# The steps ahead of the first token tile, written in another order, with x split out of PSUM

## The chip, the cores and the metric

One core of one Trainium2 chip runs the whole program. The metric is the device time of one execution in microseconds (us), the median of several. The engines are named as in the profile: PE (matrix multiply, with PEld for its weight loads), DVE (vector), ACT (scalar and activation), POOL (GpSimd), SP (the queue that issues most transfers).

## The reference

Three layers follow one another on 3072 tokens of width 512.

```
attention: q, k, v of (4, 8, 768, 64); 24 chunks of 32 queries per head; a chunk sees its own 32 keys,
           16 to the left, 8 to the right and 8 memory keys;  out = softmax(q k^T / 8) v
x    = attention out as (3072, 512)
xn   = x / sqrt(mean(x^2) + 1e-6) * rms_g
y    = (silu(xn @ w_gate) * (xn @ w_val)) @ w_out          512 -> 1536 -> 512
h    = y @ w_in;  g = h if h >= 1, 0 if h <= -1, else (h + 1)^2 / 4
out  = g @ w_out2                                          512 -> 2048 -> 512
```

## The kernel before

The tokens are worked in six tiles of 512. Attention comes in 24 units `u` (256 tokens of four heads); two units make a pair, 256 tokens of all heads, and two pairs make a tile. Matrix products are done as three passes on split numbers: every operand is a rounded part `hi` plus a rest `lo`, and `mm3` adds hi·hi, hi·lo and lo·hi. So x needs its hi (`xh`) and lo (`xl`) before the first projection, and each weight needs both too.

The change concerns the steps ahead of the first tile. They are written out by hand in the string `ORDER`, and the engines take their instructions in that order. One letter is one step, the number its unit (or its block of 128 tokens):

- `f`: idle matmuls (`fill`, L104) in that number; `s` scores on PE (L426); `m` maximum and subtraction on DVE (L439, L442); `e` exponential on ACT (L451); `a` four transposes on PE (L456); `A` their copy on ACT (L462); `v` product with v on PE (L472); `n` division on DVE (L493 to L499); `q` sums of squares on ACT (L512); `k` two small DVE operations; `p` the root, on POOL (L531); `r` the scaling by root and `rms_g` (L542); `x` four transposes (L552).
- `X` copies a transposed block from PSUM into `xn` (L565). `H` and `L` split `xn` into `xh` (ACT, L354) and `xl` (DVE, or POOL for those in `LO_ON_POOL`, L358), in eight half-tiles each. `G` and `R` are the scaling of pair 0 done by POOL (L685) and ACT (L689) in place of `r`.
- `c`, `d`, `g` convert a unit of weights: `c` reads the loaded 64-bit words on ACT (L133), `d` joins them on DVE (L143, L144), `g` writes hi on ACT (L117) and lo on POOL (L118). A unit is 128 columns of `w_gate`, `w_val`, or 128 rows of `w_out`, in that order by turns; its load (L125, 512 KB) goes through a ring of three buffers, so load n+3 waits until `d` of unit n has read its buffer.

After `ORDER` the first tile begins. For each of 12 blocks `f` of the hidden width PE does 12 matmuls for gate (L579 to L581), 12 for val, and 12 for the output of the block before. Between those groups lie three slots, and in each slot one unit of weights is converted a step further (`conv_w`). From block 1 on PE so needs a new unit about every 12 matmuls. Slots also carry the attention of later tiles. In this first tile PE and SP follow the program's order and the other engines' order is set by the tool's scheduler when the kernel is built; afterwards every engine has the written order.

Of the kernel before, what the change touches and what calls it, by code (L numbers as in the profile page):

```python
# [22 lines left out]


ORDER = """
f15 s0 m0 s1 m1 e0 e1 f4 a0 s2 A0 m2 a1 c0 d0 v0 A1 f6 v1 n0 e2 n1 s3 q0 c1 k0 m3 a2 q1 A2 G0 f4
e3 G1 c2 k1 p0 v2 f1 R1 a3 d1 A3 n2 g0 d2 x1 v3 R0 g1 X1 q2 n3 f7 k2 x0 q3 X0 f1 H4 H6 f3 k3 p1
s4 L4 r2 g2 r3 H0 x2 X2 L0 x3 H2 L6 f3 X3 m4 e4 f4 L2 H1 L1 H5 a4 H3 L5 L3 c3 H7 f1 L7 d3 A4 g3
"""
LO_ON_POOL = ('L0', 'L3', 'L4', 'L6', 'L7')  # L30

TT = 512
PT = 256
# [7 lines left out]
def tile_stream_attention_moe_moe2(  # L41
# [10 lines left out]
    nc = tc.nc  # L52
# [3 lines left out]
    KK = DM // P  # L56
# [8 lines left out]
    att = att_only.enter_context(tc.tile_pool(name="att", bufs=1, side="right"))  # L65
# [11 lines left out]
    xs = poolS("xs", 1)  # L77
# [35 lines left out]
    w1 = {}  # L113
    raw, absd, f32s = [], [], []

    def split(hi, lo, src, eng_lo):
        nc.scalar.activation(hi, src, AF.Copy)  # L117
        eng_lo.tensor_tensor(out=lo, in0=src, in1=hi.bitcast(F32), op=ALU.subtract)  # L118

    def load_w(units, n):  # L120
        for _ in range(n):
            if units:
                dst, key, src = units.pop()
                w64 = wst.tile([P, 1024], U32, tag="w64", name="w64")
                nc.sync.dma_start(w64, src)  # L125
                raw.append((dst, key, w64))
# [23 lines left out]
        join(tu, w64)  # L150
        f32s.append((dst, key, tu))

    def conv_g(eng_lo=nc.gpsimd):
        dst, key, tu = f32s.pop(0)
        w = unit(3 * key[1] + "gvo".index(key[0]))
        split(w[:, 0], w[:, 1], tu.bitcast(F32), eng_lo)
        dst[key] = (w[:, 0], w[:, 1])

    def conv_w():

        n = len(absd)
        if f32s:
            conv_g(nc.vector)
        if raw:
            conv_c()
        if n:
            conv_d()

    units1 = [(w1, ("gvo"[i % 3], i // 3), wts1[i].bitcast(U32)) for i in range(3 * F1)]
# [18 lines left out]
    tt_ = nc.vector.tensor_tensor  # L188
# [147 lines left out]
    m2 = {"single": True, "pace": 0.0, "hold": False}  # L336
# [10 lines left out]
    xhl = {}

    def x_hi(src, kk, part):
        if part.start == 0:  # L350
            xhl[kk] = [
                xs.tile([P, TT], F32R, tag=f"x{hl}{kk}", name=f"x{hl}{kk}") for hl in "hl"
            ]
        nc.scalar.activation(xhl[kk][0][:, part], src[:, kk, part], AF.Copy)  # L354

    def x_lo(src, kk, part, eng):
        hi, lo = xhl[kk]
        eng.tensor_tensor(  # L358
            out=lo[:, part], in0=src[:, kk, part], in1=hi[:, part].bitcast(F32), op=ALU.subtract
        )  # L360

    def split_x(src):
        for kk in range(KK):
            x_hi(src, kk, slice(0, TT))
            x_lo(src, kk, slice(0, TT), nc.vector)


    qk_t = {}
# [27 lines left out]
    def load_v(u):  # L396
        if u >= NU:
            return
        n = 8 * (D + 1)
        if u < 4:  # L400
            if not tails:
                tails.append(xs.tile([P, 4, 2, D + 1], F32, tag="xn", name="v_tail"))
            tail = tails[0][:, u]
            nc.sync.dma_start(tail, v[u].rearrange("p (h c) -> p h c", h=2)[:, :, n - D - 1:])
            vt = [xs.tile([P, TT], F32, tag=f"x{'hl'[hp]}{u}", name="v_in") for hp in range(2)]
            m = n - D - 1
        else:
# [98 lines left out]
    def part_q(u):  # L506
        pr, hh = divmod(u, 2)
        x = x_t[pr]
        ss = small.tile([P, 2], F32, tag="ss", name="ss")
        for blk in range(2):  # L510
            sq = att.tile([P, 4, P], F32, tag="aT", name="sq").rearrange("p g i -> p (g i)")[:, :256]
            nc.scalar.activation(  # L512
                sq, x[blk][:, hh * 256:hh * 256 + 256], AF.Square, accum_out=ss[:, blk:blk + 1]
            )
        ss_t[u] = ss
# [29 lines left out]

    def step_x(pr, blk, ps):
        t, o = divmod(pr, 2)
        if t < 2 and t not in xn_t:
            xn_t[t] = xs.tile([P, KK, TT], F32, tag="xn", name="xn")
        x = x_t[pr]  # L550
        for kk in range(KK):
            nc.tensor.transpose(ps[:, 0, kk * P:(kk + 1) * P], x[blk][:, kk * P:(kk + 1) * P], ident)  # L552
        ps_t["x", pr, blk] = ps

    def part_X(pr, blk):
        t, o = divmod(pr, 2)
# [7 lines left out]
        if pr < 2:
            nc.scalar.activation(xn, rows, AF.Copy)  # L565
        else:
            for kk in range(KK):
                nc.scalar.activation(xn[:, kk], rows[:, kk], AF.Copy, scale=g_t[:, kk:kk + 1])
# [59 lines left out]
    slots = [ps_a] + [spsum.tile([P, 2, 512], F32, name=f"ps_s{i}") for i in range(2)]  # L628
# [2 lines left out]
    load_qk(1)  # L631
    load_v(0)
    load_qk(2)
    load_w(units1, 1)
    load_v(1)
    fns = {"s": step_s, "a": step_a, "v": step_v, "m": part_m, "e": part_e, "A": part_A,
           "n": part_n, "q": part_q, "k": part_k}
    parts = {"s": "me", "a": "A", "v": "nqkp"}
    free = list(range(3))
    use = {}  # L640
    for st in ORDER.split():
        c, n = st[0], st[1:]
        if c == "f":
            fill(slots[free[0]], int(n))
            continue
        n = int(n)
        if c in "savx":
            use[c, n] = free.pop(0)
            ps = slots[use[c, n]]
            if c == "x":  # L650
                step_x(n // 2, n % 2, ps)
            else:
                fns[c](n, ps)
                if n >= 4:
                    done.add(st)
            if c == "s" and n >= 3:
                load_qk(n + 1)
            if c == "v" and n >= 3:
                load_v(n + 1)
            if st == "s0":  # L660
                load_qk(3)
                load_w(units1, 1)
                nc.sync.dma_start(g_b, rms_g.partition_broadcast(P))
                nc.sync.dma_start(g_t, rms_g.rearrange("(k p) -> p k", p=P))
                load_v(2)
                load_w(units1, 1)
                load_v(3)
        elif c == "X":
            part_X(n // 2, n % 2)
            free.append(use.pop(("x", n)))  # L670
        elif c == "r":
            step_r(n // 2, (n % 2,))
        elif c == "p":
            part_p(n)
        elif c in "HL":
            kk, o = divmod(n, 2)
            part = slice(o * PT, o * PT + PT)
            if c == "H":
                x_hi(xn_t[0], kk, part)
            else:  # L680
                x_lo(xn_t[0], kk, part, nc.gpsimd if st in LO_ON_POOL else nc.vector)
        elif c == "G":
            cols = slice(n % 2 * PT, n % 2 * PT + PT)
            for x in x_t[n // 2]:
                nc.gpsimd.tensor_tensor(out=x[:, cols], in0=x[:, cols], in1=g_b[:, cols], op=ALU.mult)  # L685
        elif c == "R":
            pr, blk = divmod(n, 2)
            x = x_t[pr][blk]
            nc.scalar.activation(x, x, AF.Copy, scale=rs_t[pr][:, blk:blk + 1])  # L689
        elif c == "c":  # L690
            conv_c()
        elif c == "d":
            conv_d()
            load_w(units1, 1)
        elif c == "g":
            conv_g()
        else:
            fns[c](n)
            if c in "mAn":
                free.append(use.pop(({"m": "s", "A": "a", "n": "v"}[c], n)))  # L700
# [448 lines left out]
    o1 = Out(F1 // 2, 0, 7, done1, xq)  # L1149
# [130 lines left out]
```

## Time and profile before

| | |
|---|---|
| runs of the kernel | 1160.21, 1160.97, 1162.92 us (median 1160.97) |
| profiled execution | 1161.3 us, its span 1159.5 us |
| mean granted clock of PE | 0.994 of full |
| PE, DVE, ACT, POOL busy, share of the span | 97%, 71%, 53%, 10% |
| first matmul of the first tile | 40.87 us after the span's start |

The span is the stretch from the first to the last instruction of the program; 1.8 us of the execution lie around it. The busy share of PE counts idle matmuls (`f`) and matmuls at a lowered clock as well.

### The profile page before, as it was taken

The numbers are of one execution on the slowest core, as the hardware profiler recorded it, in microseconds if no ns is written. First come the engines' busy times: TensorE is split into PE (matmuls) and PEld (weight loads), VectorE is DVE, ScalarE is ACT, GpSimd is POOL, SyncE is SP. The second block draws the span as 40 slices with busy tenths as digits, with TensorE's granted clock in tenths as the row PEclk, the third lists the DMA queues.
The fourth block names the chain that finished last, engine by engine and source line by source line (L and its number), as shares of the span: only waits on it lengthen the run. The fifth ranks groups of instructions, "written<-read, shape, count | busy, mean of one in ns | idle before, by whom it ended". The sixth has DMA issues, their size and how long they took to land.

```text
span 1159.5 us, 21026 instructions
## 1 busy us (share of the span) xinstructions
PE 1126.5 (97%) x7909; PEld 911.0 (79%) x7909; DVE 821.7 (71%) x1426; ACT 618.8 (53%) x1096; POOL 115.6 (10%) x165
## 2 busy tenths in 40 slices
PE   6889999999999999999999999999999999999998
PEld 4667888777877777887888888788887788887886
DVE  4777767767756666767676867897677887578855
ACT  4677656556566766444444634456444465344553
POOL 2500002223122122101110000000000000000000
PEclk9899999999999999999999999999999999999999
DMA  9766538998979787879997697766777666763564
GB/s 317 236 233 196 187 128 270 298 334 270 305 244 302 256 278 240 289 256 367 407 391 255 212 312 241 220 187 187 233 210 261 181 188 216 221 196 88 162 188 158
DMA packets 144212, 281.81 MB, mean 243 GB/s; under 512 B 15216, under 2 KB 65392, under 8 KB 142320
## 3 DMA queue, kind: packets, MB, share of 16 engines
q1 hardware_dynamic: 123664, 228.57, 60.9%
q0 software_dynamic: 12768, 43.52, 10.9%
q10 hardware_dynamic: 7680, 8.39, 2.1%
q8 instruction: 62, 1.02, 0.4%
q14 instruction: 38, 0.31, 0.1%
HBM read 201.26 MB, written 79.17 MB: 242 GB/s over the span
## 4 chain that ended last, share of the span: by engine, by line
PE 75%; DVE 7%; DMA 7%; ACT 6%; issue 3%; POOL 1%; SPq 0%; ACTq 0%; DVEq 0%; POOLq 0%
PE ps_y L1065 14%; PE ps_g L1065 11%; PE ps_g L579 5%; PE ps_g L580 5%; PE ps_g L581 5%; DMA w<-in_w_dram 3%; PE ps_g L903 3%; PE ps_b L903 3%; PE ps_b L905 3%; PE ps_b L904 3%; PE ps_g L904 3%; PE ps_g L905 3%; PE ps_y L579 3%; PE ps_y L581 2%; PE ps_y L580 2%
## 5 line engine op out<-in xcount | busy, mean ns | idle before, releaser
L1065 PE MATMUL ps_y<-r,wo 128*128 128x512 f32 x672 | 156.2, 390 | 0.0
L579 PE MATMUL ps_g<-xh,wall 128*128 128x512 f32 x384 | 155.7, 405 | 0.0
L581 PE MATMUL ps_g<-xh,wall 128*128 128x512 f32 x384 | 150.8, 393 | 0.0
L580 PE MATMUL ps_g<-xl,wall 128*128 128x512 f32 x384 | 150.6, 392 | 0.0
L1065 PEld LDWEIGHTS ps_y<-r,wo 128*128 128x128 f32 x672 | 125.7, 188 | 26.0
L1015 DVE TENSOR_TENSOR r<-h,r 128x512 fp32r<-128x512 f32 x167 | 112.0, 687 | 44.4 <-ACT r L1013 44.4
L966 ACT ACTIVATE t<-t,half 128x512 f32<-128x512 f32 x96 | 66.9, 720 | 128.3 <-DVE t L965 125.4
L1013 ACT ACTIVATE r<-h 128x512 fp32r<-128x512 f32 x167 | 100.7, 625 | 56.5 <-DVE r L1015 17.5
L1065 PE MATMUL ps_g<-r,wo 128*128 128x512 f32 x498 | 116.0, 390 | 0.0
L1065 PEld LDWEIGHTS ps_g<-r,wo 128*128 128x128 f32 x498 | 93.2, 188 | 19.4 <-DVE r L1015 0.2
L581 PEld LDWEIGHTS ps_g<-xh,wall 128*128 128x128 f32 x384 | 72.6, 189 | 15.8
L579 PEld LDWEIGHTS ps_g<-xh,wall 128*128 128x128 f32 x384 | 72.7, 189 | 15.6
L580 PEld LDWEIGHTS ps_g<-xl,wall 128*128 128x128 f32 x384 | 72.7, 189 | 13.7
L903 PE MATMUL ps_b<-wall 128*128 128x512 f32 x202 | 79.3, 392 | 0.7 <-DVE ps_g L930 0.3
L903 PE MATMUL ps_g<-wall 128*128 128x512 f32 x198 | 78.4, 396 | 1.6 <-DVE ps_y L930 0.7
L904 PE MATMUL ps_b<-wall 128*128 128x512 f32 x202 | 78.7, 389 | 0.0
L905 PE MATMUL ps_b<-wall 128*128 128x512 f32 x202 | 78.6, 389 | 0.0
L579 PE MATMUL ps_y<-hh,wall 128*128 128x512 f32 x192 | 77.6, 404 | 0.0
L904 PE MATMUL ps_g<-wall 128*128 128x512 f32 x198 | 77.1, 390 | 0.0
L905 PE MATMUL ps_g<-wall 128*128 128x512 f32 x198 | 77.1, 390 | 0.0
L581 PE MATMUL ps_y<-hh,wall 128*128 128x512 f32 x192 | 75.1, 391 | 0.0
L580 PE MATMUL ps_y<-hl,wall 128*128 128x512 f32 x192 | 74.9, 390 | 0.0
(201 smaller groups left out, 2104.6 us busy)
## 6 DMA issues: line engine op xcount, KB each, us to landing
wo<-w2o_d SPq DMA_DIRECT2D x88, 512.0 KB, 3.4
wall<-w2p_d SPq DMA_DIRECT2D x168, 256.0 KB, 2.9
wall<-w1p_d SPq DMA_DIRECT2D x84, 256.0 KB, 6.1
w<-in_w_dram SPq DMA_DIRECT2D x36, 512.0 KB, 5.1
w<-in_w_dram POOLq DMA_DIRECT2D x32, 512.0 KB, 5.5
k_in<-in_k_dram SPq DMA_DIRECT2D x48, 256.0 KB, 5.1
wo<-w1o_d SPq DMA_DIRECT2D x21, 512.0 KB, 3.5
v_in<-in_v_dram SPq DMA_DIRECT2D x40, 260.0 KB, 4.2
```

The costliest lines, as they stand in the source:

```text
L579: nc.tensor.matmul(ps, wh, xh, start=start, stop=False)
L580: nc.tensor.matmul(ps, wh, xl, start=False, stop=False)
L581: nc.tensor.matmul(ps, wl, xh, start=False, stop=stop)
L903: nc.tensor.matmul(bank, wh, xh, start=st, stop=False, skip_group_check=True)
L904: nc.tensor.matmul(bank, wh, xl, start=False, stop=False, skip_group_check=True)
L905: nc.tensor.matmul(bank, wl, xh, start=False, stop=kk == 1, skip_group_check=True)
L966: nc.scalar.activation(s, s, AF.Square, scale=0.5, bias=half)
L1013: nc.scalar.activation(r[:, 0], src, AF.Copy)
L1015: tt_(out=r[:, 1], in0=src, in1=r[:, 0].bitcast(F32), op=ALU.subtract)
L1065: nc.tensor.matmul(bank[p][m], a, b, start=s0, stop=s1, skip_group_check=True)
```

## The change

`ORDER` is a new string. Loads of all four first attention units are issued ahead of weights 2 and 3 (the first load of a weight now stands behind the loads of unit 3). The steps `X`, `G` and `R` are gone: a transposed block goes from PSUM straight to `xh` (a copy on ACT, `H`) and `xl` (a subtraction on DVE, `L`), a block of 128 tokens at a time, and pair 0 is scaled by the two `r` steps on DVE. The lo part of a weight becomes a step of its own, `o`, on DVE. POOL keeps the roots `p` and the transfers that it issues. Steps `a` and `A` of unit 4 move into the first tile. The buffers `xh` and `xl` become one tile each; v of the first four units lies in them.

```diff
 ORDER = """
-f15 s0 m0 s1 m1 e0 e1 f4 a0 s2 A0 m2 a1 c0 d0 v0 A1 f6 v1 n0 e2 n1 s3 q0 c1 k0 m3 a2 q1 A2 G0 f4
-e3 G1 c2 k1 p0 v2 f1 R1 a3 d1 A3 n2 g0 d2 x1 v3 R0 g1 X1 q2 n3 f7 k2 x0 q3 X0 f1 H4 H6 f3 k3 p1
-s4 L4 r2 g2 r3 H0 x2 X2 L0 x3 H2 L6 f3 X3 m4 e4 f4 L2 H1 L1 H5 a4 H3 L5 L3 c3 H7 f1 L7 d3 A4 g3
+f15 s0 m0 f4 s1 e0 m1 f3 a0 A0 e1 v0 n0 s2 m2 a1 A1 v1 n1 q0 e2 k0 q1 k1 p0 f2 a2 A2 s3 m3 e3 c0
+r0 f3 v2 n2 a3 A3 r1 x0 H0 d0 q2 k2 v3 n3 q3 x1 H1 k3 p1 L0 g0 f8 r2 r3 L1 x2 H2 x3 H3 s4 o0 c1
+L2 L3 d1 g1 m4 o1 e4 c2 c3 d2 g2 d3 o2 g3 o3 f4
 """
-LO_ON_POOL = ('L0', 'L3', 'L4', 'L6', 'L7')
...
-    def conv_g(eng_lo=nc.gpsimd):
+    def conv_hi():
         dst, key, tu = f32s.pop(0)
         w = unit(3 * key[1] + "gvo".index(key[0]))
-        split(w[:, 0], w[:, 1], tu.bitcast(F32), eng_lo)
+        src = tu.bitcast(F32)
+        nc.scalar.activation(w[:, 0], src, AF.Copy)
         dst[key] = (w[:, 0], w[:, 1])
+        return lambda: tt_(out=w[:, 1], in0=src, in1=w[:, 0].bitcast(F32), op=ALU.subtract)
...
-            vt = [xs.tile([P, TT], F32, tag=f"x{'hl'[hp]}{u}", name="v_in") for hp in range(2)]
+            vt = [x[:, u] for x in v4]
...
     load_qk(2)
-    load_w(units1, 1)
     load_v(1)
...
                 load_qk(3)
                 load_w(units1, 1)
+                load_v(2)
                 nc.sync.dma_start(g_b, rms_g.partition_broadcast(P))
+                load_v(3)
                 nc.sync.dma_start(g_t, rms_g.rearrange("(k p) -> p k", p=P))
-                load_v(2)
-                load_w(units1, 1)
-                load_v(3)
-        elif c == "X":
-            part_X(n // 2, n % 2)
+                load_w(units1, 2)
+        elif c == "H":
+            if not xhl:
+                xh, xl = (xs.tile([P, KK, TT], F32R, tag=tag, name=tag) for tag in ("xh", "xl"))
+                xhl.extend((xh[:, kk], xl[:, kk]) for kk in range(KK))
+            nc.scalar.activation(xh[:, :, n * P:n * P + P], rows(n), AF.Copy)
+        elif c == "L":
+            dst, hi = (x[:, :, n * P:n * P + P] for x in (xl, xh))
+            tt_(out=dst, in0=rows(n), in1=hi.bitcast(F32), op=ALU.subtract)
             free.append(use.pop(("x", n)))
...
         elif c == "g":
-            conv_g()
+            lows.append(conv_hi())
+        elif c == "o":
+            lows.pop(0)()
```

On DVE, around the scaling of pair 1 (`x_nat<-x_nat,rs,g_b`) that the last blocks of x wait for, the order before is this; L358 writes `xl`, L143 and L144 are `d`, L880 is the first product of gate and val:

```order
L521 TENSOR_SCALAR ss<-ss 128x2
L525 SCALAR_TENSOR_TENSOR ss<-ss 128x2
L542 SCALAR_TENSOR_TENSOR x_nat<-x_nat,rs,g_b 128x512 x2
L439 TENSOR_REDUCE m<-ps_s_163 128x8
L442 TENSOR_TENSOR e<-ps_s_163,m 128x2x4x64
L358 TENSOR_TENSOR xl_722<-xn,xh_721 128x256
L358 TENSOR_TENSOR xl_709<-xn,xh_708 128x256
L358 TENSOR_TENSOR xl_654<-xn,xh_653 128x256
L143 TENSOR_SCALAR tu<-tu 128x512
L144 SCALAR_TENSOR_TENSOR tu<-w_360,tu 128x512
```

The same place of the changed kernel has L657 for `xl`, L154 for the lo of a weight, L138 and L139 for `d`:

```order
L510 SCALAR_TENSOR_TENSOR ss<-ss 128x2
L657 TENSOR_TENSOR xl<-ps_s_165,xh 128x4x128
L527 SCALAR_TENSOR_TENSOR x_nat<-x_nat,rs,g_b 128x512 x2
L657 TENSOR_TENSOR xl<-ps_s_164,xh 128x4x128
L154 TENSOR_TENSOR wall<-tu,wall 128x512
L657 TENSOR_TENSOR xl<-ps_a,xh 128x4x128
L657 TENSOR_TENSOR xl<-ps_s_165,xh 128x4x128
L138 TENSOR_SCALAR tu<-tu 128x512
L139 SCALAR_TENSOR_TENSOR tu<-w_254,tu 128x512
```

All four `xl` blocks and the lo of the first weight now stand on DVE behind that scaling, and the second weight (w_254) is joined behind them; before, five of eight `xl` parts and the lo of weights were POOL's.

On ACT, at the first activation of the first tile (the one that reads `ps_g`), the order before has L133 for `c`, L117 for the hi of a weight, L868 for Silu, L594 for the hi of the product:

```order
L133 ACTIVATE tu<-w_562 128x512
L117 ACTIVATE wall<-tu 128x512
L133 ACTIVATE tu<-w_577 128x512
L868 ACT_TABLE_LOAD
L868 ACTIVATE s<-ps_g_111 128x512
L117 ACTIVATE wall<-tu 128x512
L133 ACTIVATE tu<-w_756 128x512
L117 ACTIVATE wall<-tu 128x512
L594 ACTIVATE hh<-s 128x512
```

In the changed kernel the same place reads as follows, with L128, L152, L842 and L576 for the same four:

```order
L128 ACTIVATE tu<-w_256 128x512
L128 ACTIVATE tu<-w_558 128x512
L842 ACT_TABLE_LOAD
L842 ACTIVATE s<-ps_g_111 128x512
L152 ACTIVATE wall<-tu 128x512 x2
L128 ACTIVATE tu<-w_688 128x512
L576 ACTIVATE hh<-s 128x512
L128 ACTIVATE tu<-w_703 128x512
L152 ACTIVATE wall<-tu 128x512
```

The weights before are, in their order, w_188, w_248, w_257, w_360, w_562, w_577, w_756; after, w_244, w_254, w_256, w_558, w_688, w_703, w_708. So ahead of the first Silu ACT had read six units before and reads four now, and the third and fourth unit get their hi behind that Silu (their lo stands on DVE behind the product of gate and val that follows it).

On SP, the loads behind those of the first units stand so before (L404 and L411 load v, L392 k, L393 q, L125 a weight):

```order
L125 DMA w_360<-in_w_dram 128x1024
L392 DMA k_in<-in_k_dram 128x512 x2
L393 DMA q_in<-in_q_dram 128x512
L125 DMA w_562<-in_w_dram 128x1024
L125 DMA w_577<-in_w_dram 128x1024
L411 DMA v_in<-in_v_dram 128x520 x2
L392 DMA k_in<-in_k_dram 128x512 x2
L393 DMA q_in<-in_q_dram 128x512
L125 DMA w_756<-in_w_dram 128x1024
```

And so in the changed kernel (L120 a weight, L377 k, L378 q, L396 v):

```order
L377 DMA k_in<-in_k_dram 128x512 x2
L378 DMA q_in<-in_q_dram 128x512
L120 DMA w_558<-in_w_dram 128x1024
L396 DMA v_in<-in_v_dram 128x520 x2
L377 DMA k_in<-in_k_dram 128x512 x2
L378 DMA q_in<-in_q_dram 128x512
L120 DMA w_688<-in_w_dram 128x1024
L120 DMA w_703<-in_w_dram 128x1024
```

The fifth and sixth unit (w_562, w_577) stood ahead of the loads of attention unit 5; their like (w_688, w_703) now stand behind them, and those wait until the scores of unit 4 are done.

## Rows read from the trace of the kernel before

**Rows 1.** Windows: busy us (instructions) per engine, granted PE clock, DMA share, GB/s.

```profile
25.00:28.00 3.00, 3.00 (x73) 2.05 (x72) 2.17 (x7) 2.81 (x7) 1.47 (x1) 0.50 1.03 386
31.00:35.50 4.50, 0.12 (x5) 0.00 (x0) 2.87 (x1) 1.15 (x4) 4.48 (x7) 0.97 0.97 316
36.00:41.90 5.90, 5.79 (x22) 4.24 (x22) 4.34 (x8) 4.67 (x11) 1.79 (x3) 0.50 0.15 56
60.00:80.00 20.00, 16.43 (x194) 12.82 (x193) 15.11 (x29) 13.33 (x21) 0.00 (x0) 1.00 0.71 235
```

**Rows 2.** The page: engines; a queue of instruction fetches (packets, MB, share).

```profile
PE 1126.5 (97%) x7909; PEld 911.0 (79%) x7909; DVE 821.7 (71%) x1426; ACT 618.8 (53%) x1096; POOL 115.6 (10%) x165
...
q8 instruction: 62, 1.02, 0.4%
```

**Rows 3.** The chain that ended last, 0 to 60 us: start, us, what.

```profile
13.21 1.20 issue
...
17.00 2.07 issue
...
23.45 0.67 issue
...
26.29 1.12 PE ps_s L472 x64
...
51.70 6.27 DMA w<-in_w_dram
```

**Rows 4.** Groups by line, 0 to 41 us: busy us, mean ns, idle before.

```profile
L542 DVE SCALAR_TENSOR_TENSOR x_nat<-x_nat,rs,g_b 128x512 f32<-128x512 f32 x2 | 4.2, 2154 | 1.8 <-POOL rs L531 1.8
L118 POOL TENSOR_TENSOR wall<-tu,wall 128x512 fp32r<-128x512 f32 x3 | 4.0, 1335 | 2.2 <-ACT wall L117 2.1
...
L358 POOL TENSOR_TENSOR xl<-xn,xh 128x256 fp32r<-128x256 f32 x4 | 3.3, 833 | 3.9 <-ACT xh L354 3.9
...
L462 ACT ACTIVATE aT<-ps_s 128x512 f32<-128x512 f32 x4 | 2.4, 592 | 0.7 <-PE ps_s L472 0.5 <-PE ps_s L456 0.2
...
L442 DVE TENSOR_TENSOR e<-ps_s,m 128x512 f32<-128x512 f32 x3 | 2.1, 691 | 0.1
...
L117 ACT ACTIVATE wall<-tu 128x512 fp32r<-128x512 f32 x3 | 1.9, 617 | 0.0
```

**Rows 5.** Timeline of DVE, ACT and POOL, 14 to 32 us: start, us, instruction.

```profile
14.86 0.43 DVE L143 TENSOR_SCALAR tu<-tu 128x512 uint32<-128x512 uint32 x1 [0.94 <-ACT tu L133]
15.32 0.69 DVE L144 SCALAR_TENSOR_TENSOR tu<-w,tu 128x512 uint32<-128x512 uint32 x1
...
27.55 0.17 DVE L493 TENSOR_SCALAR rd<-ps_s 128x8 f32<-128x8 f32 x1 [0.71 <-ACT wall L117]
...
27.97 0.41 ACT L512 ACTIVATE sq<-x_nat 128x256 f32<-128x256 f32 x1
27.98 0.76 DVE L499 TENSOR_TENSOR x_nat<-ps_s,rd 128x256 f32<-128x256 f32 x2
...
28.82 0.19 ACT L512 ACTIVATION_READ_ACCUMULATOR sq<-x_nat 128x1 f32 x1
...
31.88 0.71 POOL L531 TENSOR_TENSOR rs<-ss,nhalf 128x2 f32<-128x2 f32 x1
```

**Rows 6.** Timeline, 40 to 50 us: start, us, instruction, idle before it.

```profile
40.87 0.85 PE L579 MATMUL ps_g<-xh,wall 128*128 128x512 f32 x1
...
42.48 9.54 SPq L125 DMA_DIRECT2D w<-in_w_dram  x5
...
43.66 1.28 ACT L868 ACT_TABLE_LOAD   x1
...
46.57 0.66 ACT L133 ACTIVATE tu<-w 128x512 f32<-128x512 f32 x1 [0.49 <-DMA w<-in_w_dram]
...
46.99 0.39 PE L579 MATMUL ps_g<-xh,wall 128*128 128x512 f32 x1
...
49.71 0.39 PE L579 MATMUL ps_g<-xh,wall 128*128 128x512 f32 x1
```

More of the change, by code (lines that the diff above doesn't have):

```diff
@@ L114, in tile_stream_attention_moe_moe2 @@
     raw, absd, f32s = [], [], []
-    def split(hi, lo, src, eng_lo):
-        nc.scalar.activation(hi, src, AF.Copy)
-        eng_lo.tensor_tensor(out=lo, in0=src, in1=hi.bitcast(F32), op=ALU.subtract)
     def load_w(units, n):
@@ L162, in conv_w @@
         if f32s:
-            conv_g(nc.vector)
+            conv_hi()()
         if raw:
@@ L345, in tile_stream_attention_moe_moe2 @@
     bg = list(reversed(steps))
[L347 to L360, printed above, removed]
+    v4 = [xs.tile([P, KK, TT], F32, tag=tag, name="v_in") for tag in ("xh", "xl")]
+    xhl = []
     def split_x(src):
-        for kk in range(KK):
-            x_hi(src, kk, slice(0, TT))
-            x_lo(src, kk, slice(0, TT), nc.vector)
+        for kk, (hi, lo) in enumerate(xhl):
+            nc.scalar.activation(hi, src[:, kk], AF.Copy)
+            tt_(out=lo, in0=src[:, kk], in1=hi.bitcast(F32), op=ALU.subtract)
     qk_t = {}
@@ L510, in part_q @@
         for blk in range(2):
-            sq = att.tile([P, 4, P], F32, tag="aT", name="sq").rearrange("p g i -> p (g i)")[:, :256]
+            sq = att.tile([P, 512], F32, tag="e" if u < 4 else "aT", name="sq")[:, :256]
             nc.scalar.activation(
@@ L547, in step_x @@
         t, o = divmod(pr, 2)
-        if t < 2 and t not in xn_t:
+        if t == 1 and t not in xn_t:
             xn_t[t] = xs.tile([P, KK, TT], F32, tag="xn", name="xn")
@@ L563, in part_X @@
         rows = ps[:, 0, :].rearrange("p (k i) -> p k i", k=KK)
[L564 to L568, printed above, removed]
+        for kk in range(KK):
+            nc.scalar.activation(xn[:, kk], rows[:, kk], AF.Copy, scale=g_t[:, kk:kk + 1])
         if t >= 2:
@@ L639, in tile_stream_attention_moe_moe2 @@
     free = list(range(3))
-    use = {}
+    use, lows = {}, []
+    rows = lambda n: slots[use["x", n]][:, 0, :].rearrange("p (k i) -> p k i", k=KK)
     for st in ORDER.split():
@@ L674, in tile_stream_attention_moe_moe2 @@
             part_p(n)
[L675 to L689, printed above, removed]
         elif c == "c":
@@ L783, in slot @@
             after.clear()
-    xn_t.pop(0)
     pend = None
```

## The prediction

> **What bounds the kernel now.** The page comes first: PE is busy 97% of the span, the next engine 71% [rows 2]. So what a change ahead of the first tile can give is PE time that is empty or slow there, and what it can take is PE time that goes empty in the tile behind it. The first matmul of the first tile starts at 40.87 [rows 6]; the windows show an empty PE from 31.0 to 35.5 (0.12 us busy of 4.5) and a PE at 1.2 GHz, half the full clock, from 25 to 28 and again from 36 to 41.9, the second time right behind that gap [rows 1]. The chain of waits names what else holds the stretch: 1.20 us at 13.21, 2.07 at 17.00 and 0.67 at 23.45 in which PE waits for nothing that the profile shows ("issue") [rows 3]. They stand inside runs of small attention matmuls, about as many PE instructions apart each time. The page has 62 transfers in an instruction queue for 7909 matmuls and 7909 weight loads [rows 2], some 255 instructions for each, so I read these stops as PE waiting for its next block of instructions. Last, the first tile itself: from 60 to 80 PE is empty for 3.57 us [rows 1], and there the chain runs through a transfer of weights that takes 6.27 us [rows 3]. Already at 46.57 ACT waits for a load that was issued at 42.48 [rows 6]. So weights are short in that tile, and time won ahead of it need not stay won.
>
> **The blocks of instructions.** Ahead of the tile the changed PE program has as many scores and products as before, and ten idle matmuls fewer. If the blocks arrive when they did (14.4, 19.1 and 24.1, the ends of the three waits), they stop other steps: `v` of unit 0 now runs ahead of the first stop, but `s` of unit 2 meets it; the second is still near the end of `v` of unit 1, the third near the end of `v` of unit 2. So that product ends near 24.45 in both kernels, and all earlier edits (loads in another order, `A0` ahead of `e1`, unit 0's product earlier) are worth nothing for the start of the tile; the blocks cover them. Without that cover they would be worth some 4 us, which is a rival below.
>
> **From 24.45 to the tile.** Division of unit 2 takes 1.19 (27.55 to 28.74 for its like [rows 5]): 25.65. `v` of unit 3 at half clock takes 1.12 [rows 3]: 26.8. `H0` must wait for it, since x lies where v lay; it costs 0.6 (a 128x512 copy out of PSUM [rows 4]): 27.45. Squares of unit 2 are next on ACT, 1.04 (27.97 to 29.01 [rows 5]): 28.5; DVE holds its small sum ahead of unit 3's division, so that runs from 28.7 to 29.9. Squares of unit 3 start after its first half and end at 30.55, sum and root 0.2 + 0.71 [rows 5]: 31.5.
>
> Here the change gains most. Before, the two scalings behind the root took 2.15 each, while POOL ran its subtractions of 0.83 and 1.34 [rows 4]; the same form with nothing on POOL took 0.69 [rows 5]. With POOL at roots alone I take 0.69 twice: 32.9. The price of the contention is so 2 x 1.46 = 2.9 us of this path; the bounds are 0 and 2.9, and I take the upper, as the row of 0.69 is DVE alone.
>
> Then the last transposes (0.6 from 32.9), `H3` 0.6 and its `L`. DVE has L1, the lo of the first weight, L2 and L3 behind the scaling, 0.69 each [rows 4]: 32.9 + 2.8 = 35.7. Idle matmuls and scores of unit 4 fit beside that. First matmul of the tile: **35.7, 5.1 us earlier**. Of these 2.9 are the contention; the rest is that x needs no `xn` and no half-tile pieces.
>
> **What the tile gives back.** A projection is 12 matmuls, 2.72 us (46.99 to 49.71 [rows 6]). Gate of block 0 runs 35.7 to 38.4, val to 41.15 at full clock. Two queues now stand differently. DVE: join of unit 2 (0.43 + 0.69 [rows 5]) to 36.8, `m4` 1.4, lo of unit 2 at 38.9, just in time. ACT: exponential of unit 4, two reads of 0.66, a table load of 1.28 [rows 6], Silu 0.6: 42.15, then hi of the third and fourth weight: 43.4. DVE: product 42.9, two lo parts: 44.25. Block 1's gate needs the fourth weight: PE ends val at 41.15 and can't do its first matmul before 43.4, its third before 44.25. **PE waits 2.3 + 0.4**; gate ends near 46.5, where it ended at 49.7 before [rows 6].
>
> The fifth weight is issued after unit 2's join, at 36.9, lands near 41 (4.0 for the one issued at 42.48 [rows 6]) and is read at 43.4 to 44.1. But its hi stands on ACT behind the read of the sixth, issued at 40.75 and landing at 44.75. Read, hi and lo follow: 47.9. PE, after unit 4's transposes (moved in, 0.6), needs it at 47.6: 0.35 more. Val of block 1 ends at 50.2, before at 49.71 + 2.72 = 52.4. Left of the 5.1: **2.2 us**.
>
> From there the pattern is the old one: three buffers, one unit a slot. The 3.57 us of waits at 60 to 80 [rows 1] I take as unchanged; the bounds are that they vanish (-3.6) or double (+3.6), and the units' distance to PE is nearest to before's.
>
> The clock is the open term. Before, the half clock covered the tile's first 1 us and cost some 0.7 (gate and val of block 0 took 46.99 - 40.87 = 6.12 instead of 2 x 2.72 = 5.44 [rows 6]). In the new order PE has gaps of about 2.4 and 1.7 us between 27 and 33. If a low stretch like 36 to 41.9 falls on the start of the tile, its matmuls run at half rate for up to 6 us, which moves the product, and the lo parts behind it, by up to 2.4; without one nothing is lost. I take 0.5, between these. Sum: 2.2 - 0.5 = 1.7 us less. The profiled execution is 1161.3, so 1159.6; it stands 0.3 above the median of the runs, so **1159.3**.
>
> **Rivals.**
> - *Instruction blocks don't hold the new order.* Loads of units 2 and 3 arrive earlier, and if PE is not stopped, unit 1's product ends near 14.7, unit 2's near 18.5 and unit 3's near 21.5, as v of unit 3 has landed by then; the tile starts near 31.5, 4.2 earlier than in my sum, and most of it stays since the conversion steps move along: 1155.5. The three waits speak against it, the emptier DMA queue behind the first weights for it. The Trainium skill ("Runtime: NRT & Kernel Launch", section Instruction fetch mechanics) says that fetches come in 256-instruction blocks and that crossing one is mostly hidden; the trace agrees on the size, not on the hiding. By that rule this rival would hold. Chance 0.15.
> - *The weights come late: slower.* The price is the sixth weight. If it lands not 4.0 but 6.27 after its issue, as the one in the chain did [rows 3], the fifth's hi is 2.3 later and so is PE; if then the waits at 60 to 80 double, because the ring enters the tile with two units fewer ahead, 3.6 more: 2.2 - 2.3 - 3.6 is 3.7 slower, 1164.7. It decides from a landing near 47 on. For it: ACT waits for loads here already; against: the queue is idle at 40 in my order. Chance 0.20.
> - *The change doesn't end the slow scalings.* If the 2.15 is no matter of POOL's work, 2.9 of the 5.1 are gone, and the tile gives back less, about half, since its conversions stand behind the same scalings: 1160.8, within 0.2%. Against it: 0.69 for the same form. Chance 0.10.
>
> **How the numbers follow.** My case has 0.55. 0.2% of the median is 2.3 us, about what a measurement of this kernel can tell from no change; so faster means under 1158.65. My case reaches from 1157 (no low clock, a little less waiting) to 1161.5 and lies on both sides: 0.27 faster, 0.28 same. Faster 0.27 + 0.15 = 0.42; same 0.28 + 0.10 = 0.38; slower 0.20. The range goes from 1156.0 to 1163.5 and cuts the far half of the first two rivals; my case alone is 1157 to 1161.5.
>
> **What would show it.** Right: scalings (L527) of 0.7 each; first `ps_g` matmul at 34 to 37; "issue" waits in `s` of unit 2 and `v` of units 1 and 2; PE empty for 2 to 3 us ahead of block 1's gate. Wrong: "issue" waits gone and the tile at 32; L527 at 2; PE waiting for weights beyond 80, where it hardly waited before; or half clock through the tile's first 6 us.

## The result and the profile after

The changed kernel takes 1167.74 us (median of 12 runs, 1165.16 to 1173.59) against 1161.91 us before (12 runs): ratio 1.0058, 95% interval 1.0039 to 1.0076. It is slower by some 6 us, and the range forecast, 1156.0 to 1163.5, doesn't hold it. The profiled execution has a span of 1163.4 us, 3.9 more than before. A trace is of one run alone: the changed kernel's is of its fastest (1165.16 us), those of e4 and e5 below are of their slowest (1168.31 and 1167.54 us).

The page's row of engines, which answers to [rows 2], tells nothing of it:

```profile
PE 1126.7 (97%) x7899; PEld 909.7 (78%) x7899; DVE 820.4 (71%) x1433; ACT 614.3 (53%) x1086; POOL 103.1 (9%) x152
```

The windows do. Here are those of the start and one at 505 us, columns as in [rows 1]:

```profile
13.00:25.00 12.00, 8.10 (x271) 5.73 (x272) 5.36 (x14) 4.72 (x13) 0.72 (x1) 0.72 0.97 315
25.00:28.00 3.00, 1.96 (x73) 1.46 (x72) 2.24 (x5) 2.02 (x6) 0.00 (x0) 1.00 0.41 145
28.00:34.90 6.90, 5.13 (x83) 3.26 (x83) 5.68 (x13) 3.75 (x10) 1.45 (x2) 0.75 0.46 156
35.00:41.00 6.00, 5.72 (x26) 4.39 (x24) 5.15 (x10) 4.10 (x6) 1.48 (x3) 1.00 0.95 323
60.00:80.00 20.00, 16.36 (x134) 13.00 (x133) 15.03 (x30) 14.13 (x24) 1.07 (x1) 1.00 0.77 262
505.00:520.00 15.00, 10.83 (x42) 8.51 (x41) 4.38 (x9) 3.64 (x7) 1.98 (x3) 0.89 0.74 262
```

And the same last window of the kernel before:

```profile
505.00:520.00 15.00, 15.00 (x68) 12.25 (x67) 7.46 (x14) 6.18 (x12) 2.29 (x4) 1.00 0.96 348
```

From 505 to 520, far behind every step that the change moves, PE is empty for 4.2 us and at half clock for a part of the rest. The start itself went almost as forecast. PE's timeline of the changed kernel, 12 to 48 us:

```profile
14.54 0.83 PE L411 MATMUL ps_s<-k_in,q_in 64*32 64x64 f32 x61 [2.07 <-issue]
...
19.20 0.37 PE L457 MATMUL ps_a<-v_tail,aT 64*32 64x65 f32 x2 [1.15 <-issue]
...
23.95 0.26 PE L457 MATMUL ps_a<-v_in,aT 64*32 64x65 f32 x4 [0.33 <-issue]
...
34.95 0.51 PE L561 MATMUL ps_g<-xh,wall 128*128 128x512 f32 x1
...
42.25 0.50 PE L561 MATMUL ps_g<-xh,wall 128*128 128x512 f32 x1 [1.53 <-ACT wall L152]
...
43.13 0.50 PE L563 MATMUL ps_g<-xh,wall 128*128 128x512 f32 x1 [0.15 <-DVE wall L154]
...
47.12 0.50 PE L563 MATMUL ps_g<-xh,wall 128*128 128x512 f32 x1 [0.52 <-DVE wall L154]
```

The tile starts at 34.95 (forecast 35.7, before 40.87) and then waits 1.53, 0.15 and 0.52 for weights. The two scalings of pair 1, 2154 ns each before [rows 4], take 1.41 together:

```profile
31.21 1.41 DVE L527 SCALAR_TENSOR_TENSOR x_nat<-x_nat,rs,g_b 128x512 f32<-128x512 f32 x2 [0.17 <-POOL rs L516]
```

The loss is in one place. The timeline of the changed kernel at 505 us, where four tiles are through and the last two are taken up as a pair (`product`, L877; `ys` is the output of the fourth tile, `y_d` its place in DRAM):

```profile
505.35 0.32 SPq L596 DMA_DIRECT2D y_d<-ys  x1
...
505.95 0.58 ACT L896 ACTIVATE ps_g<-ps_g 128x512 f32<-128x512 f32 x1 [1.44 <-PE ps_g L879]
...
511.66 0.60 ACT L897 ACTIVATE t<-ps_b 128x512 f32<-128x512 f32 x1 [5.13 <-DMA y_d<-ys]
...
513.42 0.69 DVE L904 TENSOR_TENSOR ps_b<-t,ps_g 128x512 f32<-128x512 f32 x1
...
514.16 0.79 PE L877 MATMUL ps_g<-wall 128*128 128x512 f32 x1 [4.17 <-DVE ps_b L904]
```

The same three instructions of ACT and DVE before:

```profile
507.17 0.32 SPq L614 DMA_DIRECT2D y_d<-ys  x1
...
509.13 0.60 ACT L923 ACTIVATE t<-ps_b 128x512 f32<-128x512 f32 x1 [0.78 <-PE ps_b L905]
...
510.89 0.69 DVE L930 TENSOR_TENSOR ps_b<-t,ps_g 128x512 f32<-128x512 f32 x1
```

Read from the bottom: PE waits for DVE, DVE for ACT's copy into `t`, and ACT 5.13 us for a store to land. Before, the copy waited for nothing but its product, though the store stood at the same point of the program and landed later still (at 514.02, against 511.56 in the changed kernel). Nothing in the arithmetic ties `t` to `y_d`; what ties them is memory. The pool `xs` (xn, x, v) is closed there and the next pool lies over it. The addresses of the built programs, in bytes behind the start of `xs`, with the old tenant ahead of the bar and the new one behind it:

```
                   before                    changed
     0 to  8192    xn, ys  | r0 r1           xh      | r0 r1
  8192 to 16384    x tiles | r2 r3           xl      | r2 r3
 16384 to 24576    x tiles | r4 t0 t1        xn, ys  | r4 t0 t1
```

Places are given in the order in which buffers are first asked for. Before, that was `v_tail` (in the buffer xn) and then v of unit 0. The change asks for `v4`, the two whole tiles, first; so `xn`, and in it `ys`, moved from the front to the back, under the `t` that is handed out first:

```
        m2["n"] += 1
        return m2["t"][m2["n"] % len(m2["t"])]
...
        p5 = tmp2("p5")
        nc.scalar.activation(B, A, AF.Copy)
        nc.scalar.activation(p5, C, AF.Copy)
```

### The profile page after: what moved, and what is told of

Read it like the earlier page. It is cut to its first block, busy times and chain, and to the rows that moved or that the text cites. A ratio compares the mean times of both kernels' runs of the same rounds, so it can differ in the third digit from the quotient of the medians.

```text
span 1163.4 us, 20975 instructions
## 1 busy us (share of the span) xinstructions
PE 1126.7 (97%) x7899; PEld 909.7 (78%) x7899; DVE 820.4 (71%) x1433; ACT 614.3 (53%) x1086; POOL 103.1 (9%) x152
## 4 chain that ended last, share of the span: by engine, by line
PE 48%; DVE 5%; ACT 2%; issue 1%; DVEq 0%
PE ps_y L1039 14%; PE ps_g L1039 11%; PE ps_g L877 3%; PE ps_b L877 3%; PE ps_b L879 3%; PE ps_b L878 3%; PE ps_g L879 3%; PE ps_g L878 3%; PE ps_y L877 2%; PE ps_y L879 2%; PE ps_y L878 2%; ACT t L940 2%; DVE h L944 1%; DVE t L939 1%; PE ps_y L1075 1%; DVE t L908 1%
## 5 line engine op out<-in xcount | busy, mean ns | idle before, releaser
L877 PE MATMUL ps_g<-wall 128*128 128x512 f32 x198 | 78.9, 399 | 5.7 <-DVE ps_b L904 4.2
L877 PE MATMUL ps_b<-wall 128*128 128x512 f32 x202 | 79.5, 393 | 0.7 <-DVE ps_g L904 0.3
```

Of the source, the lines that this page charges most:

```text
L877: nc.tensor.matmul(bank, wh, xh, start=st, stop=False, skip_group_check=True)
```

## The experiments

Theory A: this placement makes the loss, and the new steps by themselves gain what was forecast. Rival B: the new steps lose the time and the wait at 505 us is only where it shows. Ratios are to runs of the kernel before on the same chip, with 95% intervals; in the expectations "the fifth run" is e5, and so on, and theories C to J are named where they come up. e8 was run once and has no ratio.

| run | median us | ratio |
|---|---|---|
| changed kernel | 1167.74 | 1.0058 (1.0039 to 1.0076) |
| e1_xn_front | 1162.53 | 0.9997 (0.9978 to 1.0016) |
| e2_t_ring | 1163.08 | 1.0006 (0.9987 to 1.0025) |
| e3_before_xn_back | 1168.45 | 1.0044 (1.0025 to 1.0062) |
| e4_lo_on_pool | 1164.16 | 1.0001 (0.9983 to 1.0019) |
| e5_v_ahead_of_x | 1160.72 | 0.9978 (0.9958 to 0.9997) |
| e6_before_v_ahead | 1160.73 | 0.9974 (0.9956 to 0.9992) |
| e7_need_order | 1161.49 | 0.9985 (0.9970 to 0.9999) |
| e9_two_more_buffers | 1159.76 | 0.9966 (0.9946 to 0.9986) |
| e10_later_tile | 1161.58 | 0.9989 (0.9970 to 1.0008) |
| e11_buffers_need | 1156.58 | 0.9943 (0.9923 to 0.9962) |
| e12_buffers_later | 1157.89 | 0.9951 (0.9933 to 0.9969) |

**e1_xn_front.** xn back in front:

```diff
+    tails = [xs.tile([P, 4, 2, D + 1], F32, tag="xn", name="v_tail")]
     v4 = [xs.tile([P, KK, TT], F32, tag=tag, name="v_in") for tag in ("xh", "xl")]
...
-    tails = []
...
-            if not tails:
-                tails.append(xs.tile([P, 4, 2, D + 1], F32, tag="xn", name="v_tail"))
```

> The changed kernel with one edit: the buffer xn (v_tail, later ys) is allocated ahead of xh and xl, as in the kernel before, so that ys no longer lies where t0 and t1 of the next pool come to lie. Theory A (placement): ACT's first copy into t1 waits no more for the last store y_d (5.13 us of ACT, 4.17 us of an empty PE and half a clock behind it near 510 us in the changed kernel); all else stays, with the first tile some 2 us ahead. Expected 1159.5 us, 1158 to 1161, ratio to before 0.998. Rival B: the loss is that of the new front steps, whose 2 us shift puts transfers later in the way, and some other wait takes the place: 1166 to 1169, as the changed kernel.

Measured: 0.9997. The copy waits 0.78 for its product, as before, and PE is busy for all of the 15 us from 505 to 520 (the timeline of SP and ACT, e1_xn_front):

```profile
505.80 0.32 SPq L594 DMA_DIRECT2D y_d<-ys  x1
...
507.76 0.60 ACT L895 ACTIVATE t<-ps_b 128x512 f32<-128x512 f32 x1 [0.78 <-PE ps_b L877]
```

The loss is gone, so rival B falls for the 5 us. But the kernel is now equal to the one before, not 2 us faster (1158 to 1161 was expected): the second half of theory A is in doubt.

**e2_t_ring.** The buffers stay as in the changed kernel; only the first `t` is another:

```diff
     second_pool(F1 // 2, 5, 5, "ring t wo h")
+    m2["n"] = 1
```

> The changed kernel with its buffers where they are, but the ring t of the next pool starts at t2 instead of t1. Theory A: the first copy writes t2, which lies over hh and not over ys; t0 and t1 come some microseconds later, when the store has landed. Expected 1159.5 us, 1158 to 1161.5, as the first run. Rival C: it is the place of the buffers as such (neighbours, banks) and not this one wait: 1166 to 1169 here, though the first run is fast. Rival B: 1166 to 1169 in both.

Measured: 1.0006. One line that touches nothing but which buffer is first gives the same as the move of the pool, and the copy waits 0.78 for its product again. It is this one wait, not the places as such (rival C falls). Like e1, it stays above what was expected, here 1158 to 1161.5 (the timeline of SP and ACT, e2_t_ring):

```profile
506.79 0.32 SPq L596 DMA_DIRECT2D y_d<-ys  x1
...
508.75 0.60 ACT L897 ACTIVATE t<-ps_b 128x512 f32<-128x512 f32 x1 [0.78 <-PE ps_b L879]
```

**e3_before_xn_back.** The kernel before, with its buffers in the changed kernel's order:

```diff
     tails = []
+    v4 = [[xs.tile([P, TT], F32, tag=f"x{hl}{u}", name="v_in") for hl in "hl"] for u in range(4)]
...
-            vt = [xs.tile([P, TT], F32, tag=f"x{'hl'[hp]}{u}", name="v_in") for hp in range(2)]
+            vt = v4[u]
```

> The kernel before with one edit: the eight tiles that hold v and then xh and xl are allocated ahead of xn, so that ys lies over t0 and t1 of the next pool, as in the changed kernel; ORDER is the old one. Theory A: the first copy into t1 waits for y_d (issued at 507, landing near 514, 6.9 us), PE goes empty for some 4 to 5 us near 512 and runs at half clock behind it: slower than before by 6 to 8 us, 1168 to 1170. Rival B: the placement costs nothing by itself: 1161.9, as before.

Measured: 1.0044, with the old ORDER untouched. Its timeline shows the same wait:

```profile
507.20 0.32 SPq L615 DMA_DIRECT2D y_d<-ys  x1
...
514.76 0.60 ACT L924 ACTIVATE t<-ps_b 128x512 f32<-128x512 f32 x1 [6.38 <-DMA y_d<-ys]
...
517.26 0.79 PE L904 MATMUL ps_g<-wall 128*128 128x512 f32 x1 [5.42 <-DVE ps_b L931]
```

The wait is there and the kernel is slower, by somewhat less than the 6 to 8 us expected. With e1 and e2 this settles the placement from both sides: taken away it is worth 5.2 us by the medians (1167.74 - 1162.53) and 7.1 by the ratios (1.0058 - 0.9997), put in 5.6 by the medians (1168.45 - 1162.85, before in those runs) and 5.1 by the ratio; so 5 to 7 us.

**e4_lo_on_pool.** e1 with POOL at work again while DVE scales:

```diff
-r0 f3 v2 n2 a3 A3 r1 x0 H0 d0 q2 k2 v3 n3 q3 x1 H1 k3 p1 L0 g0 f8 r2 r3 L1 x2 H2 x3 H3 s4 o0 c1
+r0 f3 v2 n2 a3 A3 r1 x0 H0 d0 q2 k2 v3 n3 q3 x1 H1 k3 p1 L0 g0 o0 f8 r2 r3 L1 x2 H2 x3 H3 s4 c1
...
-            lows.pop(0)()
+            lows.pop(0)(nc.gpsimd.tensor_tensor if n == 0 else tt_)
```

> The first run's kernel, with the lo of the first weight moved from DVE to POOL, so that POOL subtracts from about 31.2 us on, while DVE scales pair 1. Theory D (the slow scalings of the kernel before are POOL's work beside them): the first scaling takes 2.0 to 2.2 us instead of 0.7, the second 0.7 to 2.2 by what is left of POOL's 1.3 to 2.2 us; first matmul of the first tile 0.7 to 2 us later than in the first run (one 0.69 step less on DVE counts against it), time 0 to 1.5 us longer. Rival: the scalings were slow for another reason; they stay at 0.7 and the tile starts 0.7 us earlier.

Measured: 1.0001, and of the two scalings at 31 us the second is slow, not the first as expected. The view of the line (minimum, median and longest duration in ns, first and last start) and POOL's timeline, e4_lo_on_pool:

```profile
L525 DVE SCALAR_TENSOR_TENSOR x_nat<-x_nat,rs,g_b x4: 740/748/1758, 23.0 to 31.9; 128x512 f32<-128x512 f32 x4
```

```profile
31.28 1.80 POOL L154 TENSOR_TENSOR wall<-tu,wall 128x512 fp32r<-128x512 f32 x1
```

The scaling that starts at 31.9 takes 1758 ns and ends at 33.66, 0.58 behind POOL's end at 33.08: it stood for most of POOL's subtraction and ran then. In e1, with nothing on POOL there, both take 1.41 together. So POOL's work beside it makes a scaling slow; that the two of 2154 ns before were slow by the same is the plain reading. The Trainium skill ("SBUF — State Buffer", section Who interferes with whom) calls the ports that the two engines share an exclusive lock, over which a DVE instruction with two inputs in SBUF and a POOL instruction that reads SBUF contend; this row agrees (1758 ns behind POOL's start, some 740 for the scaling just ahead of it). The tile starts 0.8 later than in e1 (36.77 against 35.99), and the time didn't move beyond its interval of some 2 us, which can't tell 0.8 from nothing.

So the question became where the lead goes. Starts of the same large matmuls (gate, val, out, counted from the first tile's first) in the traces, in us:

| trace (its run, us) | 1st (tile) | 49th (out of block 0) | 121st (out of block 2) | 1249th (third tile) | first product of the pair |
|---|---|---|---|---|---|
| before (1161.30) | 40.87 | 53.31 | 75.99 | 383.82 | 506.21 |
| e3 (old steps, 1170.17) | 42.15 | 54.06 | 77.38 | 383.81 | 506.24 |
| e6 (old steps, 1163.50) | 40.62 | 52.54 | 78.75 | 384.06 | 506.45 |
| changed (1165.16) | 34.95 | 50.40 | 73.15 | 381.98 | 504.39 |
| e1 (new steps, 1161.99) | 35.99 | 52.22 | 74.01 | 382.46 | 504.84 |
| e2 (new steps, 1163.10) | 36.33 | 52.40 | 76.17 | 383.39 | 505.83 |
| e5 (new steps, 1167.54) | 37.87 | 53.38 | 79.39 | 388.38 | 510.82 |

Means of three and of four: the new steps are ahead by 41.21 - 36.29 = 4.9 at the tile, 53.30 - 52.10 = 1.2 at the 49th, 1.7 at the 121st (in traces that differ by 6 among themselves), and by nothing at the 1249th. But this last hangs on e5's trace: without it the lead is 5.5, 1.6, 2.9, 1.3 and, at the first product, 1.3. The trace of e4 is like e5's (390.16 at the 1249th). In these two PE waits long for ACT's copy `aT` in the attention of later tiles; here e5 and before, PE's waits from 80 to 165 us:

```profile
PE ps_a L455 <- ACT aT L445: 3.8, 2, 2.6
...
PE ps_a L472 <- ACT aT L462: 0.4, 2, 0.2
```

It is 4.6 in e4, 1.4 in e3 and e6, and 0.7 to 1.7 in the changed kernel, e1 and e2. Of e1 and e2 the lead goes behind 506 us: near 590 PE waits 1.0 and 1.5 for the weights of a product (not in the trace before, but 1.6 in e6), and the 401st product starts at 598.83 and 599.84, before at 598.05. So no single place eats the lead in all traces, and what decides it no run here shows. Two places were tried for it: a wait for v at 254 us (1.9 us before, 3.2 in e1), and the weights of the first tile.

**e5_v_ahead_of_x and e6_before_v_ahead.** The load of the next x goes behind the slot, the same edit on both sets of steps:

```diff
-            if 0 < t < NS - 1 and f == 9:
-                load_x(t + 1)
...
             slot(t, 3 * f)
+            if 0 < t < NS - 1 and f == 9:
+                load_x(t + 1)
```

> The first run's kernel (xn in front) with one more edit: the load of x for the next tile (1 MB) is issued behind the slot of its block instead of ahead of it, so the v of the next attention unit stands ahead of it in the queue. Theory E (the lead of the new front steps, 1.8 us at 237 us in the first run, is eaten at 254 us, where PE waits 3.2 us for a v that lands at a time set by the queue): v lands some 3 us earlier, the wait falls below 1 us, 2 to 3 us less: 1159.5 us, 1158.5 to 1161. Rival F: later waits for transfers (products' weights near 590 us) take the lead instead: 1162 to 1163, as the first run.

> The kernel before with the same edit alone (load of x behind the slot). Its wait for v at 254 us is 1.9 us, and 1 us of half clock follows it. Theory E: 1 to 3 us less than before, and 1 to 2 us more than the fifth run, as the lead of the new front steps counts once nothing eats it: 1160 to 1161.5. Rival F: 1162 to 1163, and no difference to the fifth run.

Measured: 0.9978 and 0.9974. The waits of PE from 240 to 262 us are empty in both, and both gain some 0.2%, which theory E said of each. That e5 would then be 1 to 2 us below e6 it also said, and that is wrong: they are equal. The lead is not what that wait ate. In e5's trace it is gone at the 121st matmul already (79.39); PE's waits ahead of that, 30 to 80 us (us in total, times, longest):

```profile
PE ps_a L439 <- ACT e L434: 5.0, 1, 5.0
...
PE ps_g L561 <- DVE wall L154: 1.4, 1, 1.4
```

**e7_need_order.** e5 with the weights in PE's order:

```diff
-    units1 = [(w1, ("gvo"[i % 3], i // 3), wts1[i].bitcast(U32)) for i in range(3 * F1)]
+    need = sorted(range(3 * F1), key=lambda i: 3 * (i // 3) + i % 3 + (i % 3 == 2) * 2.5)
+    units1 = [(w1, ("gvo"[i % 3], i // 3), wts1[i].bitcast(U32)) for i in need]
```

> The fifth run's kernel with the units of weights in the order in which PE uses them (gate, val of a block, then out of the block before) instead of gate, val, out of one block. In the first tile PE waits 1.5 + 0.7 us for weights ahead of block 1 in the changed kernel; the unit needed there is now the third, not the fourth, and the one after it the fourth. Expected: the waits for weights up to 48 us sum to 1 us instead of 2.2, no new ones; time 1 us below the fifth run if the lead lives on, else the same.

Measured: 0.9985. Waits for weights up to 48 us are 1.0, as expected, but the wait for unit 5's exponential is 5.1 (2.3 before, 2.7 in the changed kernel, 1.7 in e1). So the waits ahead of block 1 are not the bound either, as far as this trace shows; what is short comes later. ACT's timeline of e5 ahead of that exponential (L434) shows it:

```profile
68.19 0.67 ACT L128 ACTIVATE tu<-w 128x512 f32<-128x512 f32 x1 [1.13 <-DMA w<-in_w_dram]
...
70.73 0.67 ACT L128 ACTIVATE tu<-w 128x512 f32<-128x512 f32 x1 [0.83 <-DMA w<-in_w_dram]
71.42 1.28 ACT L434 ACT_TABLE_LOAD   x1
72.71 0.63 ACT L434 ACTIVATE e<-e 128x512 f32<-128x512 f32 x1
```

and the changed kernel's (L436):

```profile
65.34 0.66 ACT L128 ACTIVATE tu<-w 128x512 f32<-128x512 f32 x1 [0.41 <-DMA w<-in_w_dram]
66.02 1.28 ACT L436 ACT_TABLE_LOAD   x1
67.31 0.63 ACT L436 ACTIVATE e<-e 128x512 f32<-128x512 f32 x1
```

The exponential stands in ACT's order behind the read of a weight, and this read waits for the load. The twelfth weight lands at 62.1 us in the kernel before, at 61.9 in the changed one, 63.0 in e1 and e2, 66.3 in e5: no more than 0.2 earlier, though the tile starts earlier.

**e8_fewer_loads.** e1 without the loads of v of units 2 and 3, so that it leaves out a part of attention; one run:

```diff
+        if u in (2, 3):
+            v_t[u] = v_t[u - 2]
+            return
```

> The first run's kernel without the loads of v for units 2 and 3 (they use the v of units 0 and 1 instead, so part of attention is not computed); 1.05 MB less in the queues up to 21 us. PE's three waits for its next instructions end at 13.75, 19.23 and 25.12 us in the first run. Theory G (the instructions come behind the data in the same queues): the second and third end 1 to 3 us earlier. Rival: each takes its own time after the block before it: within 0.5 us of the first run. Also the first tile starts 1 to 3 us earlier by G.

PE's timeline, e8_fewer_loads:

```profile
12.82 0.83 PE L412 MATMUL ps_s<-k_in,q_in 64*32 64x64 f32 x61 [0.76 <-issue]
...
19.12 0.37 PE L458 MATMUL ps_a<-v_tail,aT 64*32 64x65 f32 x2 [3.30 <-issue]
```

The first stop ends 0.9 earlier than in e1, the second where it did (19.23), now after 3.30 us of waiting, and the third is gone. Neither theory gives that, and 0.9 is no more than traces differ: with all loads the first stop ends between 13.10 (e11) and 14.54 (changed), and e4 has no third stop either. The tile starts at 35.89, against 35.99, so fewer loads didn't start it earlier in this trace. What the stops wait for the traces do show: in the instruction queue a transfer of 16384 bytes ends 1.2 to 1.6 us ahead of the end of each of these stops, in every trace (at 12.84, 17.76 and 22.66 before, for 14.41, 19.07 and 24.11; at 11.49 and 17.58 in e8, for 12.82 and 19.12). In e8 the second of these starts at 16.58, in e1 at 16.73; what sets that time stays open.

**e9_two_more_buffers.** e5 with the fifth and sixth weight in xn, which the new steps leave empty in the first tile:

```diff
-                w64 = wst.tile([P, 1024], U32, tag="w64", name="w64")
+                w64 = bufs[i] if bufs else wst.tile([P, 1024], U32, tag="w64", name="w64")
...
+                wx = xs.tile([P, 2, 1024], U32, tag="xn", name="w64")
+                load_w(units1, 2, [wx[:, i] for i in range(2)])
...
-            load_w(units1, 1)
+            if s >= 2:
+                load_w(units1, 1)
```

> The fifth run's kernel (xn in front, v ahead of x) with two more buffers for weights in the first tile: the fifth and sixth unit are loaded into the buffer xn, which stands empty from the end of unit 3's product to the second tile, right behind that product; the ring of three then goes on with the seventh. Theory H (the lead of the new front steps dies in the first tile because the weights come at the pace of a ring of three: the twelfth unit lands at 62.1 us in the kernel before and at 61.9 to 66.3 with the new steps, though the tile starts 3 to 6 us earlier): the fifth and sixth land near 33 us instead of 42 to 47, the twelfth 2 to 5 us earlier than in the fifth run, PE's wait for unit 5's exponential near 70 us falls from 5.0 to below 2, and the time is 2 to 4 us less than the fifth run's, ratio to before 0.994 to 0.996. Rival I: the transfers as such are full in this stretch, so the later units land no earlier; only the waits ahead of block 1 go, time within 1 us of the fifth run, ratio 0.997 to 0.998.

Measured: 0.9966, 1 us below e5's median and not the 2 to 4 of theory H. The fifth and sixth land at 35.4 and 36.7 (45.5 and 47.3 in e5), the twelfth at 61.1 (66.3); the wait for the exponential is 3.9, not below 2. The twelfth is 5 earlier than in e5 but only 1.0 earlier than in the kernel before, so rival I has a part: two buffers more help the first weights and hardly those at 60 us. The traces can't carry more: e1 has the program of e5 in the first tile, and there the twelfth lands at 63.0 and the wait is 1.7.

**e10_later_tile.** e5 with a later start, by idle matmuls at the end of ORDER:

```diff
-L2 L3 d1 g1 m4 o1 e4 c2 c3 d2 g2 d3 o2 g3 o3 f4
+L2 L3 d1 g1 m4 o1 e4 c2 c3 d2 g2 d3 o2 g3 o3 f24
```

> The fifth run's kernel with 20 more idle matmuls ahead of the first tile, which starts some 2.9 us later (20 x 0.147). Theory H (weights set the pace in the first tile, not its start): the later start costs little, the twelfth unit lands when it did within 1.5 us, and the time is 0 to 1 us more than the fifth run's. Rival J: PE bounds the first tile and the lead is lost further on: 2 to 3 us more.

Measured: 0.9989 against 0.9978, 0.9 us more by the medians. By theory H 0 to 1, by rival J 2 to 3; the intervals of some 0.2% each don't part the two. Nor do the traces: the start is 2.0 behind e5's (39.88) but the 1249th matmul 4.7 ahead of it (383.67); beside e7, which differs from e5 in the order of weights alone, they are 2.9 and 1.3 behind (36.97 and 382.33).

**e11_buffers_need and e12_buffers_later.** e11 has the edits of e7 and e9 together on e5; e12 is e11 with the `f24` of e10.

> The run with two more buffers, and besides the weights in the order in which PE uses them. If the waits for weights in the first tile are then gone, the time is 0 to 1 us below that run; by rival I the same as the seventh run.

> The eleventh kernel (two more buffers, weights in PE's order) with 20 more idle matmuls ahead of the first tile, as in the tenth run. Theory H, carried on: with weights two units further ahead the start of the tile sets its end again, so the 2 to 3 us count: ratio to before 0.9943 + 0.0015 to 0.0025, 0.996 to 0.997, some 2 us more than the eleventh. Rival: weights still set the pace at 60 to 75 us, and the later start costs below 1 us: 0.994 to 0.995.

Measured: e11 0.9943 (0.9923 to 0.9962), 1156.58 us, the fastest here: 3 us below e9, where 0 to 1 was expected. PE's waits, 36 to 140 us, e11_buffers_need:

```profile
PE ps_a L440 <- ACT e L435: 2.6, 1, 2.6
PE ps_a L456 <- ACT aT L446: 1.6, 2, 0.9
PE ps_g L562 <- DVE wall L154: 1.0, 1, 1.0
```

On e5's 1160.72 the order alone gives nothing (1161.49), the buffers alone 1.0 us, both 4.1; why they need each other was not taken apart, and the order was not tried on the old steps, so what part the new steps have in it isn't known. e12 costs 0.0008 more by the ratios, 0.9 us, and 1.3 by the medians, for a start that was to be 2.9 later and is 4.6 later in the traces (41.16 against 36.53; at the 121st matmul 74.49 against 74.28, at the 1249th 380.54 against 377.80). That lies between the rival's "below 1 us" and theory H's 2, and inside the intervals.

## Why the prediction was wrong, step by step

- **The blocks of instructions: right.** The three stops stand in unit 2's scores and in the products of units 1 and 2, as forecast, after the same numbers of matmuls as before (221, 348, 475 in both traces), and end at 14.54, 19.20 and 23.95 (14.4, 19.1, 24.1 before). The rival in which they don't hold, with a tile at 31.5, is out.
- **From 24.45 to the tile: right.** 35.7 forecast, 34.95 in the trace and 34.95 to 37.87 in four; 5.1 us earlier forecast, 4.9 by the means. The price of the contention, 2.9, was right in size (2 x 2154 ns against 1.41 us) and, by e4's one slow scaling, in cause. The third rival is out.
- **What the tile gives back, up to block 1: right in kind, small in size.** Forecast waits of 2.3 + 0.4 and 0.35, measured 1.53 + 0.15 and 0.52. The lead there is 2.9 in the changed kernel's trace and 1.2 by the means (1.6 without e5), for 2.2.
- **"From there the pattern is the old one": it held in the changed kernel's trace, and the times don't bear it out; the smaller of two errors.** The waits at 60 to 80 were taken as unchanged, with the lead kept. In the changed kernel's trace that came out: PE is empty there for 3.64 us (3.57 before), and it is 1.8 ahead at the first product (504.39 against 506.21), close to the sum's 2.2 - 0.5 = 1.7. But with equal placement the new steps are worth nothing that can be measured: e1 against before 0.9997, e2 1.0006, the changed kernel against e3 1.0058 and 1.0044, e5 against e6 0.9978 and 0.9974. The interval of e1 alone would still hold a gain of 1.7 us; that four comparisons have none on the mean speaks against it. The lead was lost in different places (80 to 165 us, near 590 us), none of which the prediction looked at; why stays open. That weights pace the first tile is in part argued: the twelfth lands when it did. The rival "weights come late" had this mechanism, with a price of 3.7 on the wrong side that no run shows.
- **What was not in the sum at all: the larger error.** "xh and xl become one tile each" stands in the change and got no line in its cost part by part. So the step that failed is a term put at nothing without a reason. The edit moves xn by 16384 bytes, a copy at 506 us gets a store to wait for, and that costs 5 to 7 us (e1, e2, e3): 4.17 us of an empty PE, then matmuls at a clock of 0.76 on average from 515 to 520 us. No rival held it. Without it, e1 and e2 (1162.53 and 1163.08) lie inside the range forecast, but beside a kernel before of 1162.85, so not by the sum's gain. Ahead of the run, the wait could have been seen from the addresses or from what ACT waits for at that copy in both built programs; the price from the store's 6.9 us to landing (issued 507.17, landed 514.02 before), against a copy that came 2 us behind the issue.
- **The clock:** it was low ahead of the tile (0.72 on average from 13 to 25, 0.75 from 28.0 to 34.9) and not on the tile (1.00 from 35 to 41) in the changed kernel's trace; in e5 the first matmuls of the tile did run slow (0.53 from 38 to 40, matmuls 0.43 apart). The 0.5 was no more than a middle.

## What to carry to other kernels

A new shape or order of buffers is a change of its own: list what will lie over each when its pool is closed, and which store or read then stands between the old tenant and the new, however far from the edit. Time won ahead of a long stream need not reach its end: here 4.9 us at the tile were 1.2 to 1.6 at the 49th matmul, 1.3 at 506 us in three traces, and nothing in the times, while two more buffers for weights, together with the order of need, took 4.1 us off e5. That a lead counts once the weights get ahead too would fit this, but it isn't shown. A lead of a microsecond or two is to be followed in several traces: one trace of four turned it to nothing here. A stall may be tested from both sides cheaply: take it out of the new kernel in two ways and put it into the old one.

## What was not expected of the hardware

PE's three stops for instructions come after 221, 348 and 475 matmuls in the traces of both kernels, each 1.2 to 1.6 us behind the end of a transfer of 16384 bytes in the instruction queue, and PE stands for them: the second cost from 1.15 (changed) to 3.30 us (e8). The wait of 4.17 us at 510 us was followed by matmuls 0.43 us apart (514.75 to 515.18) instead of 0.23, so that the stall costs about 1.4 times its length: 5.8 us of lead were lost around it in the changed kernel's trace, from 1.8 ahead of the kernel before to 4.0 behind. In e3 it is about 1.5 times: 8.3 us lost around a wait of 5.42.
